# A second set of seven half-size products in the first layer of a retention + MLP kernel, with masks moved to ScalarE and GpSimd and two bursts placed inside the sets

## The chip, the cores and the metric

One core of one Trainium2 chip. The metric is the device time of one execution in microseconds (us), medians of several executions. All runs quoted are with a granted TensorE clock of 0.988 to 1.0. Engine names in the profile: PE is TensorE's matmul, PEld its weight load, DVE is VectorE, ACT is ScalarE, POOL is GpSimd, SP is SyncE.

## The reference

Retention (attention with a decay in place of the softmax), then a two-layer MLP with a leaky ReLU:

```python
batch, n_heads, seq, head_dim = (8, 8, 576, 64)         # q, k, v, float32
scores = scale * np.matmul(q, k.transpose(0, 1, 3, 2))
Dmat = np.where(rel >= 0, gamma[:, None, None] ** rel[None, :, :], 0.0)
attn = np.matmul(scores * Dmat[None], v)
x = attn.transpose(0, 2, 1, 3).reshape(B * S, H * D)     # 4608 tokens x 512
h = x @ w_in                                             # 512 x 2048
out = np.maximum(0.01 * h, h) @ w_out                    # 2048 x 512
```

## The kernel before

Retention runs in 36 units of 128 tokens. A unit's PE work is a "burst": 64 matmuls of 64x64 for scores and states of unit u, and for outputs of unit u-1. The MLP runs in nine groups of 512 tokens. The scheduler is off: each engine executes in the order in which the program emits its instructions.

A group's first layer has 16 blocks of 128 hidden units (`h_block`: four 512-column matmuls and a leaky ReLU on ScalarE). In groups 2 to 8 four of the 16 blocks (0, 1, 8, 9) are computed as one 2x2 block product by Strassen's scheme (Winograd's form): seven products of half size instead of eight, with sums on VectorE. The second layer is one such product (`seven`).

```python
    def masks(u):
        s16s[u] = b_pool.tile([P, 2, NP, CH], F16, name="s16")
        nc.vector.tensor_tensor(
            out=s16s[u], in0=sc_tiles[u][:, :, 0],
            in1=mask_sb.unsqueeze(1).unsqueeze(1).to_broadcast([P, 2, NP, CH]), op=MUL)

    def h_seven(g, fill):                      # product, plus, give: cut
        product("p1", w_sub(0, 0), x_sub(g, 0, 0), True)
        r["k1"] = m_pool.tile([P, 2, HT], FP, name="k1")
        nc.scalar.copy(out=r["k1"], in_=r["p1"])             # copy p1 before it is added to
        h_block(g, fill[0])
        product("p1", w_sub(0, 1), x_sub(g, 1, 0), False)    # accumulates into p1
        give(0, 0, "p1")                                     # leaky ReLU on ScalarE
        h_block(g, fill[1])
        product("p6", w_sum[:, 1], t[:, 1], True)
        plus("u2", "p6", "k1")                               # sums on VectorE
        product("p5", w_sum[:, 0], t[:, 0], True)
        plus("v", "p5", "u2")
        h_block(g, fill[2])
        product("p7", w_sum[:, 2], t[:, 2], True)
        plus("h4", "p7", "v")
        product("p5", w_sum[:, 3], x_sub(g, 1, 1), False)
        plus("h5", "p5", "u2")
        give(1, 1, "h4")
        h_block(g, fill[3])
        give(0, 1, "h5")
        product("p7", w_sub(1, 1), t[:, 3], False)
        plus("h4", "p7", "u2")
        give(1, 0, "h4")

    def burst(u, out=True):
        if u < NU:
            scores(u)                          # PE
        if out:
            outputs(u - 1)                     # PE
        if u < NU:
            masks(u)                           # VectorE
            state(u, 0)                        # VectorE, one to three operations in all
            state(u, 1)
            state_cast(u, pool_copy)           # GpSimd
        if out:
            own(u - 1)                         # ScalarE
            add(u - 1)                         # VectorE: x of unit u-1
    # step(u): burst(u), loads, then casts of unit u+2 on ScalarE and GpSimd, with the
    # four sums of x (sum_x, GpSimd) once per group, then a transposing DMA

    rest = [2, 10, 3, 11, 4, 12, 5, 13, 6, 7, 14, 15]
    for g in range(2, NG):
        more = g < NG - 1
        h_seven(g, rest[:4])
        if more:
            step(4 * g + 5)
        for n, f in enumerate(rest[4:-1]):
            h_block(g, f)
            if n == 2:
                for m in range(3):
                    mix(g, m, 0)               # VectorE: sums of the hidden layer
            if more and n == 5:
                step(4 * g + 6)
        seven(g, {0: [lambda: step(4 * g + 7)], 4: [lambda: step(4 * g + 8)]} if more else {},
              g == NG - 1, rest[-1])
```

## Time and profile before

| | before |
|---|---|
| median | 286.19 us (3 runs, 286.07 to 287.1) |
| profiled execution (its time was 287.34 us), first to last instruction | 285.6 us |
| busy PE / DVE / ACT / POOL | 97 / 70 / 51 / 48% of the span |
| a group, from the first whole block of group 2 (84.22) to that of group 8 (256.49), by six | 28.71 us |

The prediction below shows the lines. How to read them: in the chain of waits each row has start, length and what ran; if one engine's rows follow each other without holes, that engine sets the time. In a timeline a row has start, length, engine, source line, operation, output<-inputs, shape and count; a bracket tells how long the engine was idle before it and what ended that. A wait list gives microseconds in total, times, and the longest.

### The profile page before, as it was taken

What the parts mean: (1) busy time and instruction counts of PE and PEld (TensorE: products, weight loads), DVE (VectorE), ACT (ScalarE), POOL (GpSimd) and SP (SyncE); (2) the same over time, 40 slices, a digit from 0 to 9 for tenths busy, and PEclk for the clock granted to TensorE, in tenths of its full rate; (3) what the DMA queues carried; (4) which work ended last, traced back from release to release, by engine and by line L of the source; (5) the groups of instructions that cost most, each with busy time, mean ns of one, the idle gap of its engine ahead of it and who ended that gap; (6) DMA issues with size and microseconds to landing.
All of it is one profiled execution on the core that took longest, in us unless ns stands there. A gap on an engine that the chain in (4) does not pass through costs nothing.

```text
span 285.6 us, 9701 instructions
## 1 busy us (share of the span) xinstructions
PE 276.6 (97%) x4195; PEld 197.9 (69%) x4195; DVE 200.0 (70%) x335; ACT 145.5 (51%) x262; POOL 138.5 (48%) x152
## 2 busy tenths in 40 slices
PE   7789999999999999999999999999999999999994
PEld 3468888645876588658865886588658865886584
DVE  2875677987666787687768776977597659765162
ACT  4666777533237732773277426742684167316610
POOL 8959600766345527562756266626654665042000
PEclk9999999999999999999999999999999999999999
DMA  8999999999999999958596969487959451012004
GB/s 213 298 226 201 290 192 198 218 203 214 166 249 285 262 223 144 307 129 191 119 286 137 203 149 286 109 175 168 257 124 156 103 186 39 3 57 92 0 2 147
DMA packets 131739, 50.03 MB, mean 175 GB/s; under 512 B 121264, under 2 KB 126000, under 8 KB 131696
## 3 DMA queue, kind: packets, MB, share of 16 engines
q1 hardware_dynamic: 125392, 39.59, 62.3%
q0 software_dynamic: 6016, 9.70, 15.2%
q8 instruction: 33, 0.54, 0.8%
q10 hardware_dynamic: 288, 0.11, 0.1%
q14 instruction: 10, 0.08, 0.1%
HBM read 36.81 MB, written 9.44 MB: 162 GB/s over the span
## 4 chain that ended last, share of the span: by engine, by line
PE 87%; DMA 5%; DVE 3%; POOL 3%; issue 1%; POOLq 0%
PE acc L380 35%; PE acc L574 32%; PE acc L457 8%; PE acc L510 5%; POOL t L133 3%; PE sc L219 3%; DMA w_in<-in_moe_w_in_dram 3%; DMA qkT<-qk 2%; PE ot L295 2%; PE ot L306 1%; PE sc L228 1%; DVE s L237 1%; PE acc L201 0%; DVE xT L367 0%; DVE gt L554 0%
## 5 line engine op out<-in xcount | busy, mean ns | idle before, releaser
L380 PE MATMUL acc<-xT,w_in 128*128 128x512 f16 (+2 forms) x656 | 111.6, 317 | 1.1 <-DMA w_in<-in_moe_w_in_dram 0.9
L394 ACT ACTIVATE gt<-acc 128x512 f16<-128x512 f32 x123 | 71.3, 597 | 28.9 <-PE acc L380 28.8
L380 PEld LDWEIGHTS <-w_in 128*128 128x128 f16 x656 | 57.2, 98 | 33.1 <-issue 1.2
L574 PEld LDWEIGHTS <-gt 128*128 128x128 f16 x640 | 61.2, 98 | 9.5 <-ACT gt L394 0.2
L574 PE MATMUL acc<-w_out,gt 128*128 128x256 f16 x384 | 46.1, 273 | 0.0
L277 POOL CAST st<-s 128x512 f16<-128x512 f32 x21 | 13.0, 619 | 64.6 <-DVE s L261 43.7
L176 POOL TENSOR_TENSOR qk<-t,cs 128x512 f16<-128x512 f32 x28 | 31.6, 1127 | 20.7 <-ACT gt L394 14.7
L362 ACT COPY own<-ot 128x512 f32<-128x512 f32 x33 | 19.2, 582 | 41.7 <-PE ot L306 41.3
L180 POOL TENSOR_TENSOR v<-t,cs 128x512 f16<-128x512 f32 x28 | 32.8, 1170 | 2.4 <-PE acc L574 1.6
L574 PE MATMUL acc<-w_mix,gt 128*128 128x256 f16 x256 | 30.6, 273 | 0.0
L574 PE MATMUL acc<-w_mix,mix 128*128 128x256 f16 x256 | 29.3, 273 | 0.0
L173 ACT CAST qk<-t 128x512 f16<-128x512 f32 x36 | 22.3, 620 | 12.4 <-DMA t<-in_k_dram 12.3
L554 DVE TENSOR_TENSOR mix<-gt 128x1024 f16<-128x1024 f16 x16 | 13.5, 848 | 20.0 <-ACT gt L394 20.0
L574 PEld LDWEIGHTS <-mix 128*128 128x128 f16 x256 | 24.9, 98 | 3.1
L367 DVE TENSOR_TENSOR xT<-ot,own 128x512 f16<-128x512 f32 x33 | 22.5, 682 | 5.4 <-ACT own L362 5.4
L237 DVE TENSOR_TENSOR s<-sc,cs 128x512 f16<-128x512 f32 x34 | 23.2, 683 | 4.1 <-PE sc L228 4.1
L445 POOL TENSOR_TENSOR x_sum<-xT 128x512 f16<-128x512 f16 x14 | 16.2, 1155 | 3.7 <-DVE xT L367 3.7
L261 DVE TENSOR_TENSOR s<-sc,s 128x256 f32<-128x256 f32 x37 | 15.5, 418 | 2.8 <-PE sc L228 2.2
L468 DVE TENSOR_TENSOR u<-acc,k 128x512 f32<-128x512 f32 x7 | 4.8, 692 | 17.0 <-PE acc L457 14.5
L600 DVE TENSOR_TENSOR osb<-acc,u 128x512 f32<-128x512 f32 (+1 forms) x17 | 11.2, 656 | 7.9 <-PE acc L574 7.9
L445 POOL TENSOR_TENSOR x_sum<-xT,x_sum 128x512 f16<-128x512 f16 x14 | 16.2, 1154 | 0.6
L219 PEld LDWEIGHTS <-qkT 64*64 64x64 f16 x576 | 7.8, 107 | 12.4 <-issue 9.9
(74 smaller groups left out, 358.1 us busy)
## 6 DMA issues: line engine op xcount, KB each, us to landing
out_dram<-osb SPq DMA_DIRECT2D x17, 512.0 KB, 4.3
t<-in_k_dram SPq DMA_DIRECT2D x27, 256.0 KB, 3.9
t<-in_q_dram SPq DMA_DIRECT2D x26, 256.0 KB, 4.6
t<-in_v_dram SPq DMA_DIRECT2D x25, 256.0 KB, 4.4
w_in<-in_moe_w_in_dram POOLq DMA_DIRECT2D x8, 256.0 KB, 7.5
w_out<-in_moe_w_out_dram POOLq DMA_DIRECT2D x4, 512.0 KB, 10.0
t<-in_v_dram POOLq DMA_DIRECT2D x7, 256.0 KB, 5.7
t<-in_q_dram POOLq DMA_DIRECT2D x6, 256.0 KB, 6.0
```

Of the source, the lines that this page charges most:

```text
L173: nc.scalar.copy(out=qk16[u][:, 1], in_=t32[u, 1])
L176: eng.tensor_tensor(out=qk16[u][:, 0], in0=t32[u, 0], in1=decay(u, 0), op=MUL)
L180: eng.tensor_tensor(out=v16[u], in0=t32[u, 2], in1=decay(u, 1), op=MUL)
L219: nc.tensor.matmul(out=a[half(j), g, 0, p, :], lhsT=qkT[u][half(g), 1, p, half(j)], rhs=qkT[u][half(g), 0, p, half(j)], start=True, stop=T ...
L237: nc.vector.tensor_tensor(out=s16s[u], in0=sc_tiles[u][:, :, 0], in1=mask_sb.unsqueeze(1).unsqueeze(1).to_broadcast([P, 2, NP, CH]), op=MUL,)
L362: nc.scalar.copy(out=owns[u], in_=ot_tiles[u][:, :, 0:NP].rearrange("q j c t -> q c j t"))
L367: nc.vector.tensor_tensor(out=x_of(u).rearrange("q (c g) t -> q c g t", g=2), in0=ot_tiles[u][:, :, NP : 2 * NP].rearrange("q g (c j) t -> ...
L380: nc.tensor.matmul(out=hps[:, n, :], lhsT=w_in16[:, c, f * P : (f + 1) * P], rhs=xT[g][:, c, ts], start=(c == 0), stop=(c == NP - 1),)
L394: nc.scalar.activation(out=out, in_=in_, func=mybir.ActivationFunctionType.Lrelu)
L445: nc.gpsimd.tensor_tensor(out=t[:, n], in0=a, in1=b, op=SUB)
L457: nc.tensor.matmul(out=r[name][:, n, :], lhsT=lhs[:, c, n * P : (n + 1) * P], rhs=rhs[:, c, :], start=fresh and n == 0 and c == 0, stop=c ...
L574: nc.tensor.matmul(out=r[name][tb][:, 0, :] if apart else r[name][0][:, tb, :], lhsT=lhs[:, f, tb * P : (tb + 1) * P], rhs=rhs[:, f, :], s ...
```

## The change

The intent: compute four more blocks (4, 5, 12, 13) of each group by seven half-size products, which saves PE work in a kernel that PE bounds. To make room on VectorE, the masks of units 13 and later become a ScalarE copy and a GpSimd multiply; to keep bursts evenly spaced, one burst goes into the middle of each set. The first product of the second layer (`first`) becomes a filler of the second set.

```diff
-    def masks(u):
+    def masks(u, aside=False):
         s16s[u] = b_pool.tile([P, 2, NP, CH], F16, name="s16")
+        if aside:
+            nc.scalar.copy(out=s16s[u], in_=sc_tiles[u][:, :, 0])
+            nc.gpsimd.tensor_tensor(
+                out=s16s[u],
+                in0=s16s[u],
+                in1=mask16.unsqueeze(1).unsqueeze(1).to_broadcast([P, 2, NP, CH]),
+                op=MUL,
+            )
+            return
@@ h_seven
-    def h_seven(g, fill):
+    def h_seven(g, f, fill, middle=None):
@@ (h_block(g, fill[n]) becomes fill[n]() throughout)
         plus("v", "p5", "u2")
-        h_block(g, fill[2])
+        if middle is not None:
+            middle()
+        fill[2]()
@@ burst
-            masks(u)
+            masks(u, u > 12)
@@ groups (in seven: the first product becomes `first`, the rest `others`)
+        h_seven(g, 0, [block(2), block(10), block(3), block(11)], at_step(5))
+        mix(g, 0, 0)
+        mix(g, 1, 0)
+        h_seven(g, 4, [block(6), block(7), block(14), first], at_step(6))
+        mix(g, 2, 0)
+        h_block(g, 15)
+        for n in range(3):
+            mix(g, n, 1)
+        others({0: [at_step(7)], 4: [at_step(8)]} if more else {})
```

More of the change, by code (lines that the diff above doesn't have):

```diff
@@ L106 @@
     w_mix = const_pool.tile([P, 4, HF, HN], F16, name="w_mix")
-    w_sum = const_pool.tile([P, 4, NP // 2, 2 * P], F16, name="w_sum")
+    w_sum = const_pool.tile([P, 2, 4, NP // 2, 2 * P], F16, name="w_sum")
     zst = const_pool.tile([P, NP, CH], F16, name="zst")
     idle = const_pool.tile([P, TOK], F16, name="idle")
+    mask16 = idle[:, 0:CH]
     t32, qk16, v16, qkT, s16s, st16, sc_tiles, ot_tiles, xT = ({} for _ in range(9))
@@ L414, in h_unit, with w_sub, sum_w_in @@
         leaky(g_tile(g)[:, 4 * fb : 4 * fb + 4, ts], hps)
-    def w_sub(i, j):
-        return w_in16[:, 2 * j : 2 * j + 2, i * HF * P : i * HF * P + 2 * P]
+    def w_sub(f, i, j):
+        c0 = (f + i * HF) * P
+        return w_in16[:, 2 * j : 2 * j + 2, c0 : c0 + 2 * P]
     def x_sub(g, j, k):
         return xT[g][:, 2 * j : 2 * j + 2, k * HT : (k + 1) * HT]
-    def sum_w_in(n):
+    def sum_w_in(f, n):
+        t = w_sum[:, f // 4]
         a, b, op = (
-            (w_sub(1, 0), w_sub(1, 1), ADD),
-            (w_sum[:, 0], w_sub(0, 0), SUB),
-            (w_sub(0, 0), w_sub(1, 0), SUB),
-            (w_sub(0, 1), w_sum[:, 1], SUB),
+            (w_sub(f, 1, 0), w_sub(f, 1, 1), ADD),
+            (t[:, 0], w_sub(f, 0, 0), SUB),
+            (w_sub(f, 0, 0), w_sub(f, 1, 0), SUB),
+            (w_sub(f, 0, 1), t[:, 1], SUB),
         )[n]
-        nc.vector.tensor_tensor(out=w_sum[:, n], in0=a, in1=b, op=op)
+        nc.vector.tensor_tensor(out=t[:, n], in0=a, in1=b, op=op)
     x_sums = {}
@@ L445, in sum_x @@
             nc.gpsimd.tensor_tensor(out=t[:, n], in0=a, in1=b, op=SUB)
-    def h_seven(g, fill):
+    def h_seven(g, f, fill, middle=None):
         r = {}
         t = x_sums[g]
+        w = w_sum[:, f // 4]
         def product(name, lhs, rhs, fresh):
@@ L470, in give @@
         def give(i, k, name):
-            leaky(g_tile(g)[:, i * HF : i * HF + 2, k * HT : (k + 1) * HT], r[name])
-        product("p1", w_sub(0, 0), x_sub(g, 0, 0), True)
+            leaky(g_tile(g)[:, f + i * HF : f + i * HF + 2, k * HT : (k + 1) * HT], r[name])
+        product("p1", w_sub(f, 0, 0), x_sub(g, 0, 0), True)
         r["k1"] = m_pool.tile([P, 2, HT], FP, name="k1")
         nc.scalar.copy(out=r["k1"], in_=r["p1"])
-        h_block(g, fill[0])
-        product("p1", w_sub(0, 1), x_sub(g, 1, 0), False)
+        fill[0]()
+        product("p1", w_sub(f, 0, 1), x_sub(g, 1, 0), False)
         give(0, 0, "p1")
-        h_block(g, fill[1])
-        product("p6", w_sum[:, 1], t[:, 1], True)
+        fill[1]()
+        product("p6", w[:, 1], t[:, 1], True)
         plus("u2", "p6", "k1")
-        product("p5", w_sum[:, 0], t[:, 0], True)
+        product("p5", w[:, 0], t[:, 0], True)
         plus("v", "p5", "u2")
-        h_block(g, fill[2])
-        product("p7", w_sum[:, 2], t[:, 2], True)
+        if middle is not None:
+            middle()
+        fill[2]()
+        product("p7", w[:, 2], t[:, 2], True)
         plus("h4", "p7", "v")
-        product("p5", w_sum[:, 3], x_sub(g, 1, 1), False)
+        product("p5", w[:, 3], x_sub(g, 1, 1), False)
         plus("h5", "p5", "u2")
         give(1, 1, "h4")
-        h_block(g, fill[3])
+        fill[3]()
         give(0, 1, "h5")
-        product("p7", w_sub(1, 1), t[:, 3], False)
+        product("p7", w_sub(f, 1, 1), t[:, 3], False)
         plus("h4", "p7", "u2")
@@ L554, in mix, with seven @@
         nc.vector.tensor_tensor(out=z[:, fs], in0=a[:, fs], in1=b[:, fs], op=op)
-    def seven(g, hooks, last=False, block=None):
+    def seven(g, last=False):
         r = {}
-        s = sums[g]
         def product(name, lhs, rhs, fresh):
@@ L613, in give, with first, others @@
                 store(g, a, r["o", a])
-        plan = (
-            ("p1", g_part(g, 0, 0), w_part(0, 0), True, lambda: keep("k1", "p1")),
-            ("p1", g_part(g, 0, 1), w_part(1, 0), False, lambda: give(0, 0, "p1")),
-            ("p6", s[:, 1], w_mix[:, 1], True, lambda: keep("u2", "p6", "k1")),
-            ("p5", s[:, 0], w_mix[:, 0], True, lambda: keep("v", "p5", "u2")),
-            ("p7", g_part(g, 1, 0), w_mix[:, 2], True, lambda: give(1, 1, "p7", "v")),
-            ("p5", g_part(g, 0, 0), w_part(1, 1), False, lambda: give(0, 1, "p5", "u2")),
-            ("p7", g_part(g, 1, 1), w_mix[:, 3], False, lambda: give(1, 0, "p7", "u2")),
-        )
-        for n, (name, lhs, rhs, fresh, then) in enumerate(plan):
-            product(name, lhs, rhs, fresh)
-            then()
-            if n == 0:
-                if block is not None:
-                    h_block(g, block)
-                    for m in range(3):
-                        mix(g, m, 1)
-                mix(g, 3, 0)
-                mix(g, 3, 1)
-            for f in hooks.get(n, ()):
-                f()
+        def first():
+            product("p1", g_part(g, 0, 0), w_part(0, 0), True)
+            keep("k1", "p1")
+        def others(hooks):
+            mix(g, 3, 0)
+            mix(g, 3, 1)
+            for f in hooks.get(0, ()):
+                f()
+            s = sums[g]
+            plan = (
+                ("p1", g_part(g, 0, 1), w_part(1, 0), False, lambda: give(0, 0, "p1")),
+                ("p6", s[:, 1], w_mix[:, 1], True, lambda: keep("u2", "p6", "k1")),
+                ("p5", s[:, 0], w_mix[:, 0], True, lambda: keep("v", "p5", "u2")),
+                ("p7", g_part(g, 1, 0), w_mix[:, 2], True, lambda: give(1, 1, "p7", "v")),
+                ("p5", g_part(g, 0, 0), w_part(1, 1), False, lambda: give(0, 1, "p5", "u2")),
+                ("p7", g_part(g, 1, 1), w_mix[:, 3], False, lambda: give(1, 0, "p7", "u2")),
+            )
+            for n, (name, lhs, rhs, fresh, then) in enumerate(plan):
+                product(name, lhs, rhs, fresh)
+                then()
+                for f in hooks.get(n + 1, ()):
+                    f()
+        return first, others
     def keep_warm(n):
@@ L891 @@
         7: lambda: mixes(1, 2),
-        12: lambda: [sum_w_in(n) for n in range(4)],
+        12: lambda: [sum_w_in(0, n) for n in range(4)]
+        + [nc.vector.tensor_copy(out=mask16, in_=mask_sb)],
         9: lambda: early(9, 12),
@@ L899, with block, at_step @@
     burst(10)
-    seven(1, {0: [lambda: early(11, 13)], 4: [lambda: early(12, 14)]})
-    rest = [2, 10, 3, 11, 4, 12, 5, 13, 6, 7, 14, 15]
+    first, others = seven(1)
+    first()
+    others(
+        {
+            0: [lambda: early(11, 13)],
+            2: [lambda: sum_w_in(4, 0), lambda: sum_w_in(4, 1)],
+            3: [lambda: sum_w_in(4, 2), lambda: sum_w_in(4, 3)],
+            4: [lambda: early(12, 14)],
+        }
+    )
     for g in range(2, NG):
         more = g < NG - 1
-        h_seven(g, rest[:4])
-        if more:
-            step(4 * g + 5)
-        for n, f in enumerate(rest[4:-1]):
-            h_block(g, f)
-            if n == 2:
-                for m in range(3):
-                    mix(g, m, 0)
-            if more and n == 5:
-                step(4 * g + 6)
-        seven(
-            g,
-            {0: [lambda: step(4 * g + 7)], 4: [lambda: step(4 * g + 8)]} if more else {},
-            g == NG - 1,
-            rest[-1],
-        )
+        first, others = seven(g, not more)
+        def block(f):
+            return lambda: h_block(g, f)
+        def at_step(n):
+            return (lambda: step(4 * g + n)) if more else None
+        h_seven(g, 0, [block(2), block(10), block(3), block(11)], at_step(5))
[7 more added lines that the diff above has]
+        others({0: [at_step(7)], 4: [at_step(8)]} if more else {})
 _INS = ['q', 'k', 'v', 'moe_w_in', 'moe_w_out']
```

## The prediction

> **What bounds the kernel now.** I read the page's first part first: PE is busy for nearly the whole span, the other engines half to two thirds of it. A busy PE need not be a PE without waits, so next I read the chain of work that ended last, in order of time, for one group of 512 tokens (the group that starts at 198.89 us). Columns: start, length, what.
>
> ```profile
> PE 276.6 (97%) x4195; PEld 197.9 (69%) x4195; DVE 200.0 (70%) x335; ACT 145.5 (51%) x262; POOL 138.5 (48%) x152
> ```
>
> ```profile
> 198.89 0.44 PE acc L457 x4
> 199.33 0.86 PE acc L380 x4
> 200.19 0.45 PE acc L457 x4
> 200.64 0.86 PE acc L380 x4
> 201.50 0.90 PE acc L457 x8
> 202.40 0.86 PE acc L380 x4
> 203.26 0.93 PE acc L457 x8
> 204.19 0.86 PE acc L380 x4
> 205.06 0.44 PE acc L457 x4
> ...
> 206.13 5.29 PE acc L380 x24
> ...
> 216.28 7.09 PE acc L574 x64
> ```
>
> L457 are the half-size products of the first layer, L380 whole blocks, L574 the second layer. Every piece is PE, each starts where the last ended, and the same list repeats with a period of 28.7 us from 83.79 to 256.05. So groups 2 to 8 (seven of them) are bound by PE's issue alone; a four-matmul product takes 0.44 us and a block 0.86. Only the pair at 203.26 is some 0.06 over 0.87, the trace of a short wait. Other engines cost nothing here unless they make PE wait.
>
> Hence the third view, the timeline of DVE and ScalarE (ACT) just after the last product of such a set (it is issued until 205.42):
>
> ```profile
> 205.09 0.60 ACT L394 ACTIVATE gt<-acc 128x512 f16<-128x512 f32 x1
> 205.42 0.32 PE L219 MATMUL sc<-qkT 64*64 64x64 f16 x16
> 205.59 1.37 ACT L394 ACTIVATE gt<-h 128x512 f16<-128x512 f32 x2
> 205.60 0.69 DVE L468 TENSOR_TENSOR h<-acc,u 128x512 f32<-128x512 f32 x1 [0.57 <-PE acc L457]
> 206.86 0.57 ACT L362 COPY own<-ot 128x512 f32<-128x512 f32 x1
> ```
>
> DVE starts its last sum 0.18 us after PE moves on and takes 0.69; the second of ScalarE's two activations follows it and ends at 206.96; ScalarE's next instruction starts at 206.86, 1.44 us after PE moved on. In the kernel before this harms nobody: PE goes on to a burst and six independent blocks.
>
> **What the Trainium skill says.** "TensorE: Matmul & The Clock Gate", section Back-to-back issue gap, gives N/2.4 + 2.5 ns between warm matmuls, 109 ns for 256 columns and 216 for 512. The trace agrees (7.09/64 = 111 ns, 0.86/4 = 215), and its other figure there, 131 ns sustained for 512, is not seen. So seven products save work but not one half. "PSUM — Partial Sum Buffer", section Engine vs sequencer instructions: the queues of ScalarE, VectorE and GpSimd are strict FIFO, and matmuls complete in program order. The trace agrees: in the lines above ScalarE's copy `own` starts only when the activation held by DVE is through, though its own matmuls (L306) were issued by 206.06. "GPSIMD Engine Reference", section Specifications: GpSimd cannot read PSUM. The page's rows agree (no POOL row reads sc, ot or acc), which is why the moved mask needs a ScalarE copy before it.
>
> **The change, part by part.**
>
> 1. First layer, blocks 4, 5, 12, 13 of each group: 4 x 4 matmuls of 512 columns go, 4 x 0.865 = 3.46 us; 7 x 4 of 256 come, 0.44+0.45+0.87+0.93+0.44 = 3.13 us as in the existing set. Saving 0.33 us per group, 7 x 0.33 = 2.3 us. It is on PE, so on the path. If nothing else changed: 286.2 - 2.3 = 283.9.
>
> 2. VectorE gains five sums per group (5 x 0.69 = 3.5 us) and loses four masks (4 x 0.68 = 2.7). ScalarE loses four activations of PSUM (0.60), gains four (three from SBUF, 0.63), one copy `k1` (0.585) and four mask copies: about +3.0 per group. GpSimd gains four multiplies at about 1.155 each (the row of x_sum, the same shape) = 4.6. By the busy sums of a group (DVE 21.3, ACT 15.1, POOL 15.2 to 16.1 of 28.7) all stay under the period, POOL at about 20. No engine becomes the bound by its sum. The four more sums of weights and one cast (about 2.6 us on VectorE, once) lie in group 1 beside 1.75 us products with slack.
>
> 3. **Order.** The two sets now follow each other with nothing between. The second set begins: product p1, block 6, then p1 accumulated further. That third piece may not start before `k1` has copied p1 out of its bank. `k1` stands in ScalarE's queue behind the last activation of the first set, which needs VectorE's last sum, which needs the first set's last product. Let T be when PE has issued that product. By the lines above: sum T+0.18 to T+0.87, activation from T+0.91, next ScalarE instruction from T+1.44, copy of 0.585 done at T+2.02, PE resumes at about T+2.07. PE has work for 0.44 + 0.865 = 1.31 us only. So it waits **0.76 us**, in every one of seven groups, and that is more than twice what the group saves. The built program's order confirms that the third piece waits for that ScalarE copy and that the copy is behind the activation.
>
> 4. **Burst in the first set.** A burst now lies between p5 and p7. Counting from the set's start: p6, p5 are issued by 3.48, burst to 4.12, block to 5.09 (0.11 more after a burst, as 212.06 to 213.03 shows), p7 5.53, p5 5.97, block 6.83, then p7 again, which needs VectorE to have read p7 (sum h). Scores are complete at about 3.48+0.45+0.05; ScalarE copies the mask 3.98 to 4.56; VectorE's state operations wait for that copy in the built order, start at 4.6, take 0.33, 0.78 or 1.25 us for one, two or three operations, then the add of x (starts every 0.60), then h (0.69). h is done at 6.4, 6.7 or 7.15. Only three operations are late: PE waits 0.36. Which units have three follows from the chunk number modulo 9 and 4: for the unit in the first set (13, 17, 21, 25, 29, 33) the counts are 1, 2, 3, 2, 2, 3. So 2 x 0.36 = 0.7 us. The backlog this leaves on ScalarE (its last activations run one after another from about 6.7) also delays `k1`: with the same spacing (0.52 per activation) PE's wait of step 3 becomes 0.88 with two operations and 0.97 with three. Sum of step 3: 0.76 + 0.88 + 0.97 + 0.88 + 0.88 + 0.97 + 0.76 (last group, no burst) = 6.1 us.
>
> 5. Second set: its burst is followed by `first`, a 1.75 us product, so h has 0.9 us to spare; the mixes of VectorE are due before the second layer's p6 with about 0.5 us to spare. I count nothing, and 0.3 us in all for restarts after waits.
>
> Sum: -2.3 + 6.1 + 0.7 + 0.3 = +4.8; 286.2 + 4.8 = **291.0 us**. These latencies are from the trace; the timetable made of them is an estimate.
>
> **Rivals.**
> (a) The FIFO wait does not bite, and PE stays gapless: 283.9. For it: PE is gapless now, and the first layer's existing set shows only 0.06 of wait. Against: there a set is never preceded by a set, and in the trace `k` starts about 0.5 us after p1 begins because ScalarE is idle.
> (b) GpSimd becomes the late one: mask 1.155, cast 0.62, then query, x sums, value in one queue. For: the x sum needed by p6 was ready about 0.5 us early before (second sum at 229.57, p6 at 230.06). Against: before, POOL waited 2.6 us for the state there, which came after a VectorE mask of 0.68; now the state comes earlier and the mask fills the idle time. If it bites, add up to 0.5 us per group, to 294.
> (c) Transfers: the transpose of q and k takes 3.8 us to land, and bursts are now spaced about 7.2, 5.4, 7.7, 7.6 us instead of 5.9, 4.2, 7.7, 10.9. Evenly spaced bursts help; waits for qkT were 1.2 us in all. The saving in masks on VectorE gains nothing, as VectorE was hidden.
>
> **Range and chances.** The saving is nearly certain; the waits of step 3 follow from queue order, but their size could be 0.4 to 1.2 us a group. That gives 286.7 to 292.5, and rival (b) stretches the upper end: 287.0 to 293.5. Slower by over 2% begins at 291.9, 0.9 above my sum: chance 0.28. Faster by over 2% (280.5) is out of reach even of rival (a): 0.02. Within 2%: 0.70.
>
> **What the profile after would show.** Right: the period of groups at 29.3 to 29.8 us instead of 28.7; once per group a PE gap of 0.7 to 1.0 us at the second piece of p1 in the second set, released by ScalarE's `k1`; ScalarE's `k1` preceded by an activation released by VectorE; in groups 4 and 7 a further gap of some 0.4 us before the last product of the first set, released by VectorE; PE busy down in share, POOL up to about 60%. Wrong: a period of 28.4 without gaps (rival a), or gaps released by POOL or DMA (rivals b, c). A ScalarE that starts `k1` sooner than 1.44 us after the set's last product would make step 3 wrong; gaps after the second set's burst would make step 5 wrong.

## The result, and the profile after

The changed kernel takes 294.76 us (median of 6 runs, 293.98 to 295.23) against 286.16 us of the kernel before in the same rounds. The ratio is 1.0289, with a 95% interval of 1.0265 to 1.0313. Such ratios are the mean time of one kernel's fast runs over that of the other's of the same rounds, so they differ a little from the quotient of the medians. The change makes the kernel 2.9% slower.

The page's engine line, then PE's waits (who waited <- for whom: us in total, times, longest), both of the changed kernel:

```profile
PE 276.3 (95%) x4279; PEld 205.0 (70%) x4279; DVE 211.7 (73%) x352; ACT 158.3 (54%) x292; POOL 160.7 (55%) x175
```

```profile
PE acc L470 <- ACT k L488: 5.1, 7, 0.7
PE acc L470 <- DVE h L481: 1.6, 3, 1.0
...
PE acc L470 <- POOL x_sum L457: 0.3, 1, 0.3
```

PE's busy time hardly fell, but its share of the span did. (L470 is a product of a set, L390 a whole block, L481 a sum of a set, L488 the copy `k1`.) Seven waits for `k1`, one per group, are new. The next timeline is of group 2 of the changed kernel, around the border of its two sets; it answers to the lines around 205.42 of the kernel before:

```profile
90.06 1.36 ACT L404 ACTIVATE gt<-h 128x512 f16<-128x512 f32 x2
90.07 0.69 DVE L481 TENSOR_TENSOR h<-acc,u 128x512 f32<-128x512 f32 x1 [0.46 <-PE acc L470]
...
90.23 1.03 PE L390 MATMUL acc<-xT,w_in 128*128 128x512 f16 x4
...
91.33 0.57 ACT L488 COPY k<-acc 128x512 f32<-128x512 f32 x1
...
91.94 0.60 PE L470 MATMUL acc<-xT,w_in 128*128 128x256 f16 x4 [0.69 <-ACT k L488]
```

The first set's last sum (DVE, 90.07), its activation (the second of the two from 90.06), the copy (91.33) and PE's next product (91.94) form one chain. PE's block starts at 90.23 and is issued in 0.865 us, so PE stood from 91.10 to 91.94: 0.84 us. (The profile brackets 0.69, as it counts from the modelled end of the last matmul.) The wait was foreseen in place and size.

What was not foreseen is the size of a second wait and the place of a third. In group 4, inside the first set:

```profile
146.75 1.16 POOL L240 TENSOR_TENSOR s<-s,idle 128x512 f16<-128x512 f16 x1
...
147.10 1.08 DVE L275 TENSOR_TENSOR s<-stmp,cs 128x256 f32<-128x256 f32 x1
...
148.71 0.68 DVE L481 TENSOR_TENSOR h<-acc,v 128x512 f32<-128x512 f32 x1
...
149.44 0.61 PE L470 MATMUL acc<-x_sum,w_in 128*128 128x256 f16 x4 [1.02 <-DVE h L481]
```

A state operation of VectorE (L275) with both inputs in SBUF takes 1.08 us instead of its usual 0.42. It began while GpSimd ran the moved mask multiply (L240), which reads SBUF too, and it ended 0.28 us after that multiply. So did all five L275 of this trace that began inside such a multiply: they began 0.35 to 0.87 us after its start, took 1.08 to 0.56 us, and ended 0.28 us after its end. The end of the multiply, and not their own start, set theirs. The sum `h` behind the one in group 4 was late and PE waited. In group 7 the order was reversed by 0.04 us, and there GpSimd is the one that takes longer:

```profile
236.94 0.42 DVE L275 TENSOR_TENSOR s<-stmp,cs 128x256 f32<-128x256 f32 x1
236.98 1.41 POOL L240 TENSOR_TENSOR s<-s,idle 128x512 f16<-128x512 f16 x1
```

And between the sets and the second layer of every group but the last (group 4 shown), the same happens to a mix:

```profile
161.08 0.69 DVE L569 TENSOR_TENSOR mix<-gt 128x1024 f16<-128x1024 f16 x1 [0.59 <-ACT gt L404]
...
161.60 1.18 POOL L240 TENSOR_TENSOR s<-s,idle 128x512 f16<-128x512 f16 x1 [2.51 <-ACT s L239]
...
161.81 1.53 DVE L569 TENSOR_TENSOR mix<-mix,gt 128x1024 f16<-128x1024 f16 x1
...
162.29 3.90 PE L588 MATMUL acc<-w_mix,mix 128*128 128x256 f16 x32
```

In all six groups this mix ended 0.55 us after the multiply. The 32 matmuls that read the mix are listed with 3.90 us; in the kernel before the same 32 are listed with 3.66:

```profile
217.97 3.66 PE L574 MATMUL acc<-w_mix,mix 128*128 128x256 f16 x32
```

The Trainium skill has the rule, in "SBUF — State Buffer", section Who interferes with whom: a VectorE instruction with two SBUF inputs contends with a GpSimd instruction that reads SBUF, and the shared pair of ports is an exclusive lock. The pair of groups 4 and 7 agrees with it; the prediction had not used it. The kernel before shows such pairs too, at places where PE does not wait for them: here a mix takes 1.42 us instead of 0.69, and GpSimd's own row, begun beside the mix before it, 1.49 instead of 1.04.

```profile
208.38 1.49 POOL L176 TENSOR_TENSOR qk<-t,cs 128x512 f16<-128x512 f32 x1
209.00 1.42 DVE L554 TENSOR_TENSOR mix<-mix,gt 128x1024 f16<-128x1024 f16 x1
```

**Where the time went.** I read PE's issue times through groups 2 to 8 and took as a wait what a piece starts later than the piece before it needs (0.865 us for a block, 0.44 for a product, 3.50 for the 32 matmuls on the mix).

| per execution, us | predicted | trace |
|---|---|---|
| saving of the half-size products | -2.3 | -2.9 (what remains of the balance) |
| waits for `k1` (0.84 in groups 2 and 8, 0.91 in five) | +6.1 | +6.2 |
| waits for `h` in the first set (0.13, 1.18, 0.06, 0.35, 0.59 in groups 3 to 7) | +0.7 | +2.3 |
| waits for the second half of the mix (0.22 in six groups) | 0 | +1.3 |
| wait for a sum of x on GpSimd (group 5) | 0 | +0.4 |
| wait for activations in group 8 | 0 | +0.4 |
| restarts | +0.3 | not seen apart |
| sum from the first block of group 2 to the end | +4.8 | +7.7 |

The last row of the trace: from the first whole block of group 2 to the end, the changed kernel took 292.02 - 82.94 = 209.08 us, the kernel before 285.57 - 84.22 = 201.35. The medians differ by 8.6, so 0.9 us is not placed. The part before group 2 varies by itself: in the 14 profiles of this study that first block starts between 82.63 and 85.14 us. I compare kernels therefore also by the period of a group, the mean of six from the first whole block of group 2 to that of group 8: 28.71 us before, 29.84 after.

### The profile page after: what moved, and what is told of

The parts are those of the page before. It is cut to its first block, busy times and chain, and to the rows that moved or that the text cites. A ratio compares the mean times of both kernels' runs of the same rounds, so it can differ in the third digit from the quotient of the medians.

```text
span 292.0 us, 9901 instructions
## 1 busy us (share of the span) xinstructions
PE 276.3 (95%) x4279; PEld 205.0 (70%) x4279; DVE 211.7 (73%) x352; ACT 158.3 (54%) x292; POOL 160.7 (55%) x175
## 4 chain that ended last, share of the span: by engine, by line
PE 69%; DVE 16%; ACT 8%; DMA 2%; issue 2%; POOL 2%; DVEq 0%; ACTq 0%; POOLq 0%
PE acc L588 27%; PE acc L390 19%; PE acc L470 12%; ACT gt L404 6%; PE acc L525 5%; DVE mix L569 5%; DVE h L481 3%; PE sc L220 2%; DMA t<-in_q_dram 2%; DVE s L271 1%; DVE xT L377 1%; DVE s L275 1%; ACT k L488 1%; DVE v L481 1%; PE sc L229 1%
## 5 line engine op out<-in xcount | busy, mean ns | idle before, releaser
L390 PE MATMUL acc<-xT,w_in 128*128 128x512 f16 (+2 forms) x544 | 88.7, 304 | 0.3 <-DVE xT L377 0.2
L404 ACT ACTIVATE gt<-acc 128x512 f16<-128x512 f32 x102 | 60.0, 597 | 17.9 <-PE acc L390 16.3
L390 PEld LDWEIGHTS <-w_in 128*128 128x128 f16 x544 | 46.3, 98 | 17.4 <-issue 0.3
L240 POOL TENSOR_TENSOR s<-s,idle 128x512 f16<-128x512 f16 x23 | 27.3, 1186 | 41.9 <-ACT s L239 41.9
L239 ACT CAST s<-sc 128x512 f16<-128x512 f32 x23 | 13.4, 584 | 36.1 <-PE sc L229 36.1
L404 ACT ACTIVATE gt<-h 128x512 f16<-128x512 f32 x42 | 25.9, 628 | 12.4 <-DVE h L481 11.8
L181 POOL TENSOR_TENSOR v<-t,cs 128x512 f16<-128x512 f32 x28 | 30.1, 1076 | 1.7 <-DMA t<-in_v_dram 1.4
L481 DVE TENSOR_TENSOR u<-acc,k 128x512 f32<-128x512 f32 x14 | 9.7, 691 | 26.6 <-PE acc L470 26.6
L470 PEld LDWEIGHTS <-w_sum 128*128 128x128 f16 x224 | 21.9, 98 | 9.1 <-issue 0.5
L470 PEld LDWEIGHTS <-w_in 128*128 128x128 f16 x168 | 15.9, 97 | 15.6 <-issue 7.1
L377 DVE TENSOR_TENSOR xT<-ot,own 128x512 f16<-128x512 f32 x33 | 22.5, 682 | 4.9 <-ACT own L372 4.9
L481 DVE TENSOR_TENSOR h<-acc,u 128x512 f32<-128x512 f32 x28 | 19.2, 685 | 8.4 <-PE acc L470 8.4
L470 PE MATMUL acc<-x_sum,w_sum 128*128 128x256 f16 x168 | 22.9, 272 | 0.3 <-POOL x_sum L457 0.3
```

The costliest lines, as they stand in the source:

```text
L181: eng.tensor_tensor(out=v16[u], in0=t32[u, 2], in1=decay(u, 1), op=MUL)
L240: nc.gpsimd.tensor_tensor(out=s16s[u], in0=s16s[u], in1=mask16.unsqueeze(1).unsqueeze(1).to_broadcast([P, 2, NP, CH]), op=MUL,)
L377: nc.vector.tensor_tensor(out=x_of(u).rearrange("q (c g) t -> q c g t", g=2), in0=ot_tiles[u][:, :, NP : 2 * NP].rearrange("q g (c j) t -> ...
L390: nc.tensor.matmul(out=hps[:, n, :], lhsT=w_in16[:, c, f * P : (f + 1) * P], rhs=xT[g][:, c, ts], start=(c == 0), stop=(c == NP - 1),)
L404: nc.scalar.activation(out=out, in_=in_, func=mybir.ActivationFunctionType.Lrelu)
L470: nc.tensor.matmul(out=r[name][:, n, :], lhsT=lhs[:, c, n * P : (n + 1) * P], rhs=rhs[:, c, :], start=fresh and n == 0 and c == 0, stop=c ...
```

## The experiments

Theory A: `k1` is late because it stands in ScalarE's queue behind an activation that waits for VectorE's last sum of the first set. Theory B: the rest (waits for h, mix and x sum) comes from the moved masks, whose GpSimd multiply blocks VectorE, and from the amount of VectorE work in front of `h`. Rivals: the waits only move elsewhere; or the moved masks alone make the loss. Each kernel gave a correct result except where said.

| run | edit to the changed kernel | median us | before, same rounds | ratio (95%) | group period |
|---|---|---|---|---|---|
| changed kernel | none | 294.76 | 286.16 | 1.0289 (1.0265 to 1.0313) | 29.84 |
| e1 | k1 first | 287.96 | 286.15 | 1.0092 (1.0016 to 1.0168) | 28.91 |
| e2 | all masks on VectorE | 295.30 | 286.15 | 1.0307 (1.0273 to 1.0341) | 30.05 |
| e3 | no GpSimd multiply (wrong result) | 292.22 | 286.15 | 1.0198 (1.0163 to 1.0233) | 29.53 |
| e4 | kernel before, masks moved | 286.90 | 286.15 | 1.0010 (0.9979 to 1.0040) | 28.77 |
| e5 | states and add late | 300.26 | 285.99 | 1.0480 (1.0434 to 1.0526) | 30.63 |
| e6 | e1 + e5 + two masks back | 286.88 | 285.99 | 1.0021 (0.9989 to 1.0053) | 28.81 |
| e7 | e1 + e5 | 288.98 | 285.99 | 1.0094 (1.0058 to 1.0129) | 29.18 |
| e8 | e1 + e5 + all masks back | 289.04 | 285.99 | 1.0092 (1.0056 to 1.0127) | 29.08 |
| e9 | e1 + only the add late, only in the first set, + two masks back | 284.22 | 286.02 | 0.9933 (0.9920 to 0.9945) | 28.31 |
| e10 | e9 + third burst split | 284.32 | 286.02 | 0.9939 (0.9923 to 0.9954) | 28.38 |
| e11 | e9 with all masks back | 285.36 | 286.02 | 0.9985 (0.9968 to 1.0002) | 28.57 |
| e12 | e9 with all masks moved | 287.67 | 286.03 | 1.0040 (1.0002 to 1.0079) | 28.64 |

### e1: k1 in front of the activations

```diff
         nc.scalar.copy(out=r["k1"], in_=r["p1"])
+        if held is not None:
+            held()          # give(0, 1, "h5"), give(1, 0, "h4") of the first set, mix(g,0,0), mix(g,1,0)
         fill[0]()
```

> The changed kernel with one reordering: ScalarE's two last activations of the first set (and the two mixes that need them) are emitted after the second set's copy k1, so k1 no longer stands behind the sum of VectorE. Theory A (queue order makes the k1 wait): PE's wait of 0.84 to 0.91 us at the second piece of p1 vanishes in all seven groups, 6.2 us in all, and the time falls from 294.8 to about 288.6. Rival (the wait only moves to the next product, because the activations are late for something else): the time stays above 292.

Measured: 287.96 us (287.54 to 291.62; one of four runs, at a granted clock of 0.988, is 3.3 us above the next, hence the wide interval). No wait for `k1` is left in PE's list. Group 4, ScalarE and PE at the border of the sets:

```profile
148.92 0.59 ACT L488 COPY k<-acc 128x512 f32<-128x512 f32 x1
149.40 1.15 ACT L404 ACTIVATE gt<-h 128x512 f16<-128x512 f32 x2
```

```profile
148.66 1.03 PE L390 MATMUL acc<-xT,w_in 128*128 128x512 f16 x4
149.56 0.60 PE L470 MATMUL acc<-xT,w_in 128*128 128x256 f16 x4
```

The copy now runs ahead of the two activations, and the product starts 0.90 us after the block, which needs 0.865. Theory A is shown: the order of one queue cost 6.8 us of the medians, about what the table gives for `k1`. The rival falls; the other waits stayed as they were (1.0 us for h in group 4, 0.3 for the x sum).

### e2 and e3: the masks

e2 calls `masks(u)` for all units. e3 leaves out the GpSimd multiply, so the mask isn't applied (relative error 0.51). Its output is wrong, which doesn't matter for the time.

> The changed kernel with all masks on VectorE, as in the kernel before. Theory B (GpSimd's mask multiply blocks VectorE's two-input operations through a shared SBUF port): the operation L275 never takes over 0.5 us, the second-half mix 0.69 instead of 1.53, PE's mix wait (0.22 us in six groups) and the x_sum wait (0.4 us once) go, but VectorE's 0.68 of mask inside the first set raises PE's wait for h to about 0.5 us (two state operations) and 0.95 (three), 3.6 in all instead of 2.3. Sum within 1 us of the changed kernel, 293.8 to 295.8. Rival (moving the masks off VectorE is what pays): 2 us or more slower, over 297.

> Wrong result on purpose: the GpSimd multiply of the mask is left out, the ScalarE copy stays. Theory B: L275 back to 0.42 us in group 4, the second-half mix to 0.69, the mix and x_sum waits of PE gone, the wait for h down by about 0.7 us: 1.3 + 0.4 + 0.7 = 2.4 us, to about 292.4. Rival (GpSimd's multiply is hidden; the waits come from ScalarE's copy and the number of operations on VectorE): no change, 294.8 within 0.5. The k1 wait of 0.84 to 0.91 us stays in either.

e2: 295.30 us, 0.5 us above the changed kernel's median and within what theory B expected. In the view of a source line, the durations of L275 (least/median/most, ns), first of the changed kernel, then of e2:

```profile
L275 DVE TENSOR_TENSOR s<-stmp,cs x16: 424/425/1216, 14.1 to 255.2; 128x256 f32<-128x256 f32 x16
```

```profile
L275 DVE TENSOR_TENSOR s<-stmp,cs x16: 424/425/428, 13.6 to 256.1; 128x256 f32<-128x256 f32 x16
```

None is long in e2. (The longest of the changed kernel, 1.216 us, stands at 58.56, before the masks move, beside another GpSimd multiply, L181; the kernel before has one of 1.294 there. Those beside the moved multiply took 0.56 to 1.08.) But the 0.68 us of mask now stand before `h`: PE's wait for h rises from 1.6 to 3.3 us in the wait list, and the wait for `k1` from 5.1 to 5.5. The wait for an x sum was to go and did not: it stands in group 6 instead of group 5, with 0.4 us. Moving the masks neither won nor lost time in this arrangement; it exchanged one wait for another.

e3: 292.22 us, 2.5 less than the changed kernel; expected were 2.4. The second operation of the mixes, in the changed kernel and then in e3:

```profile
L569 DVE TENSOR_TENSOR mix<-mix,gt x16: 678/692/1530, 56.3 to 279.1; 128x1024 f16<-128x1024 f16 x16
```

```profile
L563 DVE TENSOR_TENSOR mix<-mix,gt x16: 677/692/692, 56.7 to 277.6; 128x1024 f16<-128x1024 f16 x16
```

None is long any more, the mix wait is gone, and the wait for `k1` is unchanged at 5.1 us. So the multiply on GpSimd, an instruction that no one on PE's path waits for by itself, costs 2.5 us of the medians. By PE's issue times the mixes are 1.3 us of it and `h` 0.7, both through VectorE (a new wait of 0.4 us for a transposing DMA in group 2 of e3 works the other way). This shows theory B's port part by its effect, but also its limits. Of the waits for `h`, 1.6 us are left: 0.60 in each of groups 4 and 7 and 0.14 in groups 3, 5 and 6, so most of them do not come from the multiply. The wait for an x sum is still there too, 0.3 us in group 6; as in e2, the multiply is not its cause alone, and the cause stays open. The L275 of the groups are all back to 0.42 us; the one at the start, beside L181, still takes 1.218.

### e4: the moved masks alone, on the kernel before

> The kernel before with only the masks of units 13 and later moved to ScalarE and GpSimd. Theory: PE bounds that kernel without waits and the masks are hidden on either engine, so 286.2 within 0.7 us, although some two-input operations of VectorE get longer. Rival (the moved masks by themselves cost what the changed kernel lost): 288 or more.

Measured: 286.90 us, ratio 1.0010: no difference. The mixes are longer there too (the second operation has a mean of 1293 ns, 961 before), but PE waits 0.2 us for them in all. So the moved masks are not what made the change slow by themselves; they cost where the new arrangement leaves no slack. The rival falls.

### e5: states and add after h5

The state operations and the add of the bursts inside both sets are emitted after `h5`, in front of the set's last sum. The casts of unit u+2 on ScalarE and GpSimd, which follow a burst, move with them.

> The changed kernel with the state operations and the add of a burst inside a set emitted after the sum h5 instead of before h; nothing else, k1 still behind the activations. Theory: PE's wait for h (2.3 us in all) goes, but the 0.8 to 1.3 us of states and 0.6 of add now stand before the set's last sum, and k1 stands behind that sum, so the k1 wait grows by about 0.9 us in the six groups with bursts: -2.3 + 5 = +2.7, about 297.5 us. Rival (the k1 wait is set by ScalarE's own backlog and not by VectorE's last sum): k1 wait unchanged, 292.5.

Measured: 300.26 us, slower than the 297.5 expected, in the expected direction. PE's wait list of e5:

```profile
PE acc L470 <- ACT k L488: 10.1, 7, 2.0
PE acc L589 <- DVE mix L570: 2.6, 4, 1.0
```

The wait for `k1` doubled, although ScalarE has no more to do: what stands before VectorE's last sum delays `k1`. As a ScalarE cast moved too, the time alone does not refute the rival of a ScalarE backlog; the trace does for this run, as in groups 3 to 7 ScalarE stood idle for 0.43 to 0.96 us until VectorE's last sum was done, and ran its activation and `k1` right after. In the changed kernel itself ScalarE has no such hole in these groups: there VectorE's sum and ScalarE's own activations end almost together (in group 4 the activations some 0.07 us later). The expectation missed the second line: states that are late in the second set also push back the mixes.

### e6, e7, e8: all repairs, with three places for the masks

All three have k1 first and states and add (and casts, as in e5) late in both sets. e6 keeps only the masks of the two bursts inside sets on ScalarE and GpSimd (`u % 4 in (1, 2)`), e7 all, e8 none.

> k1 first, states and add late inside the sets, and masks on ScalarE and GpSimd only for the two bursts inside the sets (the other two on VectorE, so that no GpSimd multiply runs beside the mixes or before the x sums). Theory: the four waits (k1, h, mix, x sum) were all that the change lost, so what is left is the saving of 0.33 us in seven groups: 283.9 to 284.5, ratio 0.992 to 0.994 to the kernel before. Rival (the new arrangement has further costs, for instance more transitions between product sizes): no faster than 286.

> As e6 but with all masks from unit 13 on ScalarE and GpSimd as in the change. Theory: the GpSimd multiply of the third burst again delays the second-half mix (PE waits 0.22 us in six groups) and the x sum in one or two groups (0.4): about 1.7 us slower than e6, 285.6. Rival (no port effect): equal to e6.

> As e6 but with all masks on VectorE: ScalarE and GpSimd are relieved, VectorE does the mask where the states were. Theory: with the states late, the mask of 0.68 us fits between v and h, so no wait for h: equal to e6 within 0.5 us, 283.9 to 284.7; the moved masks were not needed. Rival (VectorE without the move is too full for the second set): PE waits for h or k1 again, 286 or more.

e6 took 286.88 us and missed its 284. Its group 5 had almost no waits and took 28.42 us, but its mean period is 28.81: the late states of the second set crowd into VectorE's time before the second layer (PE waits 0.8 us for the second layer's v). e7 is 2.1 us slower than e6, near the 1.7 expected, and PE waits for mixes again; but its list has four such waits of 2.6 us in all, the longest 1.0, and not 0.22 in each of six groups. e8 was to equal e6 and was 2.2 us slower: its waits are spread over v (1.0 us), x sums (0.6) and a mix (0.4), so I take it that with this order VectorE has no room for all masks. These runs pointed to the remedy: take from the path before `h` as little as will do, and nothing in the second set, where a 1.75 us product already gives slack.

### e9 to e12: only the add late, only in the first set

```diff
         if out:
             own(u - 1)
+            if late:                        # the burst inside the first set
+                return lambda: add(u - 1)   # emitted after plus("h5", ...)
             add(u - 1)
-            masks(u, u > 12)
+            masks(u, u > 12 and u % 4 in (1, 2))
```

together with e1's edit. e10 moves the third burst's states between the second layer's u2 and v, and its add and the casts behind it after v; e11 puts all masks on VectorE; e12 moves all masks of units 13 and later.

> k1 first, only the add of x (not the states) late and only in the first set's burst, masks on ScalarE and GpSimd only in the two bursts inside the sets. Theory: k1 wait 0, h wait only in group 4 (some 0.4), no mix wait, at most 0.4 for the second layer's v where the third burst has three operations, x sum 0.3 once: 1.5 us of waits against a saving of 2.1 (a group without waits took 28.42 us in the run with all repairs mixed): 285.3, between 284.6 and 286.2, ratio about 0.997. Rival (something else holds PE): 286.5 or more, as in the run with all repairs mixed.

> As e9, and the third burst's states are emitted after the second layer's sum u2 and its add after v, so that PE never waits for v. Theory: 0.4 to 0.8 us less than e9, about 284.6. Rival (v was never late in e9): equal to e9 or slower, as the x sums start later.

> As e9 with all masks on VectorE. Theory: in the first set 0.68 us of mask now stand before h: PE waits for h 0.2 to 0.8 us in five groups, about 2.5 in all, 287 to 288. Rival (the moved masks are worth nothing once the add is late): equal to e9.

> As e9, but all masks from unit 13 on ScalarE and GpSimd as in the change: it differs from e9 only in the masks of the third and fourth burst of a group, and from e1 only in the late add. Theory: the GpSimd multiply beside the mix costs PE 0.22 us in six groups (1.3) and the x sum 0.4 once: 284.2 + 1.7 = 285.9, between 285.2 and 286.6; against e1's 288.0 the late add saves about 2. Rival (the place of those two masks does not matter): 284.2.

**e9 beats both kernels**: 284.22 us (283.71 to 284.6), 0.7% faster than the kernel before (less than the 2% at which a run is called faster, but clear of the noise) and 3.6% (284.22/294.76) below the changed kernel's median. It was better than expected (285.3). VectorE and PE in group 4, where the changed kernel lost most:

```profile
145.07 0.68 DVE L481 TENSOR_TENSOR h<-acc,v 128x512 f32<-128x512 f32 x1
145.67 0.68 DVE L481 TENSOR_TENSOR h<-acc,u 128x512 f32<-128x512 f32 x1
146.27 0.68 DVE L377 TENSOR_TENSOR xT<-ot,own 128x512 f16<-128x512 f32 x1
```

```profile
145.02 1.03 PE L390 MATMUL acc<-xT,w_in 128*128 128x512 f16 x4
145.88 0.60 PE L470 MATMUL acc<-x_sum,w_in 128*128 128x256 f16 x4
```

The add (L377) stands behind both sums, and the product at 145.88 follows the block without a wait. The period of 28.31 us is 0.40 below that of the kernel before: this is the saving that the change was made for, 2.8 us in seven groups (the medians differ by 1.8).

Group 4 of e9 also had luck. These are the state operation and the moved multiply, first of e9, then of e10, which has the same first set:

```profile
144.72 0.42 DVE L275 TENSOR_TENSOR s<-stmp,cs 128x256 f32<-128x256 f32 x1
144.80 1.37 POOL L240 TENSOR_TENSOR s<-s,idle 128x512 f16<-128x512 f16 x1
```

```profile
146.65 1.16 POOL L240 TENSOR_TENSOR s<-s,idle 128x512 f16<-128x512 f16 x1
...
147.01 1.08 DVE L275 TENSOR_TENSOR s<-stmp,cs 128x256 f32<-128x256 f32 x1
```

In e9 VectorE came first by 0.08 us and PE did not wait for `h`; in e10 and e12 the multiply came first and PE waited 0.59 us there. The late add alone does not remove this wait.

e10 equals e9 within the noise: the second layer's v was not late in e9 (the rival of that run). e11 is 1.1 us slower, less than the 2.5 expected; PE's wait for h there is 0.7 us in its list. e12 took 287.67 us (286.35 to 288.7), more than the 285.9 expected. Its period, 28.64, is 0.33 above that of e9, 2.0 us in six groups where 1.7 was expected; the rest of its excess lies before group 2, where the profiled execution shows a single PE wait of 1.8 us for a transposing DMA, which no theory here is about. Of the 2.0 us, the six waits for the mix make 1.4 and group 4's wait of 0.59, which e10 has as well, most of the rest. So the place of the two masks outside the sets is worth about 1.4 us. By the period the late add is worth 28.91 - 28.64 = 0.27 us a group, 1.6 us in six groups, less than the 2 expected.

## Why the prediction was wrong

**Step 1, the saving: right, a little small.** The trace gives 2.9 us and e9's period 0.40 us a group, against 0.33. The 3.13 us for seven products came from rows of the old set, and one of them (0.93) holds the short wait of 0.06 that the prediction itself had seen there. In e9's second set of group 4 the seven were issued in 3.05 us (less 0.09 before the burst), and four blocks of 0.863 less 3.05 make 0.40.

**Step 2, no engine becomes the bound by its sum: right, but not enough.** POOL rose to 55%, DVE to 73%. The step left out that GpSimd's new instructions lengthen VectorE's: a duration was taken from a row and assumed to hold beside any other work.

**Step 3, the queue order: right in place, cause and size.** It foresaw 0.76 to 0.97 us per group and 6.1 in all; the trace has 0.84 to 0.91 and 6.2, and e1 took it away with 6.8 us. That groups with three state operations would wait longer than those with two did not show: all five have 0.91.

**Step 4, the burst in the first set: right in place, mis-sized.** It foresaw 0.7 us in groups 4 and 7 alone; measured are 2.3 in five groups. Two things were missed. The first is the timetable: in e3, without the multiply, PE still waits 0.60 us in groups 4 and 7, against 0.36, and 0.14 in groups 3, 5 and 6, against none. Group 7 shows where it was short: the mask's copy started 4.14 us after the set's first product, not 3.98, and the three state operations kept VectorE for 1.33 us, not 1.25. (The extra 0.1 us that a burst costs PE lies before the burst, where p6 and p5 take 0.97 us instead of 0.87; the prediction put it after.) The second is the lock: in group 4 the state operation beside GpSimd's multiply took 1.08 us instead of 0.42, and the wait was 1.18. In group 7 the lock fell the other way, and the 0.59 is the timetable's alone. In group 6 the sum v itself started 0.36 us later than in other groups; the profile puts that down to PE, e1 and e3 do not show it, and no run tells why.

**Step 5, "I count nothing" after the second set: wrong.** This is the step that failed outright. The mixes were to be due with 0.5 us to spare. The moved mask of the third burst runs on GpSimd at that moment and makes one mix take 1.53 us instead of 0.69, and PE waits 0.22 us in six groups. A further 0.4 us for activations in the last group was not foreseen either.

**Rival (b)** was taken as a matter of GpSimd's own queue, and was argued away by its idle time. As such it showed in one group (the x sum, 0.4 us), and that wait, in group 6, outlived the multiply in e2 and e3. Its larger effect, through VectorE, was not among the rivals. **Rivals (a) and (c)**: (a) fell; it is what e9 reaches when the waits are taken away. (c) made no difference in the groups.

The sum was thus 2.9 us too small within the groups: +1.6 for h, +1.3 for the mix, +0.8 for x sum and activations, -0.6 for the saving, -0.3 for restarts and +0.1 for `k1`. With 0.9 us that isn't placed, it put the time above the range.

## What to carry to other kernels

When a pattern with a copy in it is repeated back to back, look at what stands in front of that copy in its engine's queue: here one copy behind two activations cost more than twice what the new products saved, and emitting it earlier cost nothing that the runs show. Before moving work to GpSimd, list which two-input VectorE operations will run beside it and give them the longer duration, above all where PE waits for them; which of the two comes first can hang on less than 0.1 us, as in group 4 of e9 and e10. And where PE is without holes, judge a change by the period of its steady part, which here ranged from 28.31 to 30.63 us and told kernels apart that differ by tenths, while the start of the program varied by 2.5 us.

## What the Trainium skill lacked or had wrong

- "SBUF — State Buffer", section Who interferes with whom, was right and should have been used. It gives no size for this pair; the runs show a 128x256 fp32 `tensor_tensor` at 1.08 us instead of 0.42, a 128x1024 fp16 one at 1.53 instead of 0.69, and, where VectorE began 0.04 us earlier, the GpSimd multiply at 1.41 instead of 1.16. VectorE's rows ended 0.28 us (of 0.42) and 0.55 us (of 0.69) after the multiply, so all but some 0.14 us of an operation waited.
- "TensorE: Matmul & The Clock Gate", section Back-to-back issue gap: its 131 ns sustained for 512 columns is not seen in any run here; 512-column matmuls followed each other at 215 ns, which agrees with its formula for an isolated matmul.
- "Perfetto Trace Analysis", section Optimization Strategy, says that a gap that repeats can mean too few buffers. The gap of 0.84 to 0.91 us that repeated here once per group had another cause, the order of ScalarE's queue, and went away with reordering alone (e1); that passage does not name this cause.
